# Second-half value products of a fused attention kernel in three float16 terms, with scales from a pass over v

## The chip, the cores and the metric

The kernel runs on one core of a Trainium2 chip. The metric is the device time of one execution in microseconds, lower being better; the time before is the median of three runs. The page and the trace come from one more execution, taken by the profiler. Engines are named as in the profile: PE (TensorE, matmuls), PEld (its weight loads), DVE (VectorE), ACT (ScalarE), POOL (GpSimd), SP (SyncE, which issues the transfers).

## The reference

Three stages follow each other. Causal attention over 4 batches, 8 heads, 576 positions and 64 columns per head, with a bias from a running sum; then two feed-forward layers over all 2304 tokens, with 512 columns:

```python
scores = scale * q @ k.T
cum = cumsum(maximum(s, 0))
scores = where(causal, -1e9, scores + minimum(-(cum_i - cum_j), 0))
attn = softmax(scores)                       # sum + 1e-9 below
x = attn @ v                                 # value product
h = x @ w_in                                 # 512 -> 2048
y = (s * relu(h)**2 + b) @ w_out             # 2048 -> 512
out = ((y @ w_a) * (y @ w_b)) @ w_out2       # 512 -> 1536 -> 512
```

Inputs and outputs are float32. The kernel keeps that precision by splitting operands into a high part and the rest, and by summing the products of the parts.

## The kernel before, in words

**Tiling of attention.** Heads are taken in pairs, 16 pairs for the 4 batches (`B` = 4, `NPAIR` = 4). Each pair has a first half, its first 256 query rows, which see two blocks of 128 keys (`first_half`, two pairs in each call), and a second half, its last 320 rows, which see all five blocks (`second_half`, L709). For a half, PE computes the scores, DVE takes the row maxima, ACT the exponentials, and `split_p` (L527) scales p by the reciprocal of its sum and splits it into two float16 parts. SP then issues transposes of the parts into the tile `tr`, and `value_product` (L562) multiplies.

**The value product.** v is split by `split_v` (L356) into three bfloat16 parts, p has two float16 parts. Of the six products of parts five are formed (L575), for the two heads of the pair side by side, each head in 64 of the 128 output columns. A second half has five blocks of keys with 320, 320, 320, 192 and 64 query columns, so 5 x 5 x 2 = 50 matmuls. ACT copies the sum out of PSUM, scaled back by the constant 1/32768 (L588), and DVE forms the rest (L590): the two parts of x, the input of the first feed-forward layer. The last 64 rows of each second half go to DRAM (L594) and are read back as a chunk of their own (L825).

**The first feed-forward layer.** Tokens come in nine chunks of 256: chunks 0 to 3 from the first halves, 4 to 7 from the second halves of the four batches, and chunk 8 of the short rows. Chunks 0 to 6 run as units of h (L862) and y (L882); the last two run together as `hh` (L915) and `yy` (L927). x has room for two chunks, so chunk c+2 is written where chunk c stood. The weights w1 come in 16 slices of 1 MB (L448), which ACT and DVE decode and split (L452 to L474) while the first chunks run.

**What sets the order.** All work is declared as operations with an engine, a cost and a priority (`Plan.op`, L76). `Plan.order` (L122) plays a list schedule: at each moment an engine takes the ready operation with the lowest priority number, if its buffers have room. Feed-forward matmuls have 1000 added to theirs, so attention goes first on PE and the units of h and y fill up; their element-wise work has 1000 taken off and goes first on ACT and DVE. The result is a fixed order for each engine's queue, SP's included; on the chip each queue runs in that order and waits where an input is late.

**Buffers around the change.** The tiles of the first halves (pool `att0`) are given up before those of the second halves (pool `att1`) are opened: `barrier` (L665) makes `second` (L669) follow every operation on a tile of the first pool, and the loads of the second halves (L717 to L719) come `after=opened`. In `att1` most tiles have one buffer: the raw k, q and v, the parts `vt` (L701), the transposed p (L705) and two of the three split-p tiles (L703). For each second half the parts of v are made by two ACT casts (L363) and two DVE subtractions (L365, L367).

Of the kernel before, what the change touches and what calls it, by code (L numbers as in the profile page):

```python
# [19 lines left out]
P = 128  # L20
N = 256
MASK = -1.0e30
PSC = 32768.0
G_ACT = (0, 1)
# [211 lines left out]
def fused_kernel(  # L236
# [82 lines left out]
    def make_const():  # L319
        nc.gpsimd.memset(as32(ident), 0.0)  # L320
        nc.gpsimd.affine_select(
            out=ident, in_=as32(ident), pattern=[[-1, P]], compare_op=ALU.not_equal, fill=1.0, base=0,
            channel_multiplier=1,
        )
        nc.gpsimd.memset(as32(mask1), 0.0)
        nc.gpsimd.affine_select(
            out=mask1, in_=as32(mask1), pattern=[[-1, P]], compare_op=ALU.is_ge, fill=MASK, base=0,
            channel_multiplier=1,
        )
        for i in range(0, P, SL):  # L330
            nc.gpsimd.tensor_copy(mask2[i : i + SL], as32(mask1[0:SL, 0:SL]))
# [3 lines left out]
    mask2 = atc.tile([P, SL], F32R, name="mask2")  # L335
    sb_s = const.tile([P, 1], F32, name="sb_s")
# [17 lines left out]
    t_raw = tag("att0", [P, 2, DM, 2], U32, 1, "rl")  # L354

# [134 lines left out]
    for f in range(NF1):  # L490
        if f == 1:
            sums_hl = Buf(t_w, "sums_hl")
        w1_t[f] = Buf(t_w, f"w1_{f}")
        split_w(raws[f], w1_t[f], w1[f], f % 2 == 1, W1_POS(f) - (2 * M if f >= NF1 - 3 else 0.0), W1_POS(f) - 12.0, last_rows[3:4])
        if f + 3 < NF1:
            raw_of(f + 3)
    for i in range(4, 2 * B):
        light_load(i, False)
# [62 lines left out]

    def value_product(b, half, p, vt, vap, tr, pr):  # L562
# [6 lines left out]
        xl = Buf(t_xl, f"xl{b}{p}") if half else None  # L569
        ws = [320, 320, 320, 192, 64] if half else [256, 128]  # L570

        def go():
            t = tr.t.rearrange("p (k a h q) -> p k a h q", a=2, h=2, q=nq)
            for j, w in enumerate(ws):
                for m, (vi, a) in enumerate(((0, 0), (1, 0), (2, 0), (0, 1), (1, 1))):  # L575
                    for h in range(2):
                        nc.tensor.matmul(  # L577
                            ap.t[64 * h : 64 * h + 64, :w], vap(j, h, vi), t[:, j, a, h, :w],
                            start=j == 0 and m == 0, stop=j == nkt - 1 and m == 4,
                        )  # L580

        cost = sum(5 * max(2 * w / 4.8 + 6, 58) for w in ws) / 1e3
# [4 lines left out]
        for x_, o, n in parts:  # L587
            op(ACT, ACT_PS(n), pr, lambda x_=x_, o=o: nc.scalar.activation(x_.t[:, 0], o(), AF.Copy, scale=1.0 / PSC),  # L588
               r=[ap], w=[(x_, 0)])
            op(DVE, DVE_PS(n) + 0.05, pr, lambda x_=x_, o=o: nc.vector.scalar_tensor_tensor(  # L590
                out=x_.t[:, 1], in0=o(), scalar=1.0 / PSC, in1=as32(x_.t[:, 0]), op0=ALU.mult, op1=ALU.subtract
            ), r=[ap, (x_, 0)], w=[(x_, 1)])
# [71 lines left out]

    def barrier(fn, prio):  # L665

        return op("X", 0.0, prio, fn, after=[o for o in plan.ops if any(b.tag in barrier.tags for b in o.bufs)])
# [5 lines left out]
    barrier.tags = {t_kq0, t_rv0, t_vt0, t_p0, t_tr0, t_raw, *t_hl0.values(), *t_sm0.values()}  # L673
# [27 lines left out]
    t_vt = tag("att1", [P, 5, 2, 3, D], BF16, 1, "vt")  # L701
# [7 lines left out]
    def second_half(b, p, pos):  # L709
# [27 lines left out]
        split_v((vt, lambda a: vt.t[..., a, :]), (rv, lambda: rv.t), ACT, 0.7, 0.82, pos + 0.9)  # L737
# [225 lines left out]
    def third():  # L963
# [6 lines left out]
        o for o in plan.ops if any(b.tag in att_tags or b is sets or b is masks for b in o.bufs)  # L970
# [563 lines left out]
```

## Time and profile before

| what | value |
|---|---|
| median of three runs | 1002.34 us (1001.72 to 1002.38) |
| the profiled execution | 998.96 us |
| its span in the trace | 997.2 us |
| instructions | 17243 |

The span is the time from the first to the last instruction of the profiled execution; its own time lies 1.76 us above it. In the rows below, times inside the trace count from the span's start. A group of instructions is given as line, engine, operation, output and input with their shapes, the count, then its busy time in us and the mean of one in ns, then the idle time of the engine just before and what ended it. In a chain row the first number is the start, the second the duration.

### The profile page before, as it was taken

The numbers are of one execution on the slowest core, as the hardware profiler recorded it, in microseconds if no ns is written. First come the engines' busy times: TensorE is split into PE (matmuls) and PEld (weight loads), VectorE is DVE, ScalarE is ACT, GpSimd is POOL, SyncE is SP. The second block draws the span as 40 slices with busy tenths as digits, with TensorE's granted clock in tenths as the row PEclk, the third lists the DMA queues.
The fourth block names the chain that finished last, engine by engine and source line by source line (L and its number), as shares of the span: only waits on it lengthen the run. The fifth ranks groups of instructions, "written<-read, shape, count | busy, mean of one in ns | idle before, by whom it ended". The sixth has DMA issues, their size and how long they took to land.

```text
span 997.2 us, 17243 instructions
## 1 busy us (share of the span) xinstructions
PE 968.4 (97%) x6664; PEld 871.5 (87%) x6664; DVE 707.4 (71%) x1151; ACT 548.9 (55%) x1025; POOL 108.5 (11%) x135
## 2 busy tenths in 40 slices
PE   5798999999999999999999999999999999999998
PEld 4698999999999999999988887888888888888888
DVE  6887644578888788888576627778688776878852
ACT  4788984568778777777463423344253421334431
POOL 4121000100000000000001004133143311000000
PEclk9999999999999999999999999999999999999999
DMA  9969423457776858777560103446366556977013
GB/s 240 231 164 227 163 82 79 113 128 141 168 148 157 172 128 165 159 153 146 106 226 1 63 24 125 156 147 247 137 240 228 187 185 260 377 307 253 22 65 104
DMA packets 159249, 160.12 MB, mean 161 GB/s; under 512 B 115008, under 2 KB 126016, under 8 KB 153280
## 3 DMA queue, kind: packets, MB, share of 16 engines
q1 hardware_dynamic: 159168, 159.03, 55.9%
q8 instruction: 52, 0.85, 0.4%
q14 instruction: 29, 0.24, 0.1%
HBM read 95.20 MB, written 37.52 MB: 133 GB/s over the span
## 4 chain that ended last, share of the span: by engine, by line
PE 92%; DMA 3%; DVE 2%; ACT 1%; issue 0%; POOL 0%; SPq 0%; DVEq 0%; POOLq 0%; ACTq 0%
PE b L1100 21%; PE y L882 16%; PE h L862 15%; PE pb L1324 11%; PE av L577 6%; PE hh L915 4%; PE yy L927 4%; PE bc L1100 3%; PE s L627 3%; PE s L779 3%; PE pbc L1384 2%; DMA raw<-in_w_dram 2%; DMA tr<-hl 1%; DVE x1d L1035 1%; PE s L628 0%; DMA yr<-y_dr 0%
## 5 line engine op out<-in xcount | busy, mean ns | idle before, releaser
L882 PE MATMUL y<-g,w 128*128 128x256 f32 x1344 | 183.6, 286 | 1.8 <-ACT p L643 1.8
L862 PE MATMUL h<-x_all,w 128*128 128x256 f32 x1344 | 179.0, 285 | 2.7 <-ACT x_all L588 2.1
L862 PEld LDWEIGHTS h<-x_all,w 128*128 128x128 f32 x1344 | 167.8, 192 | 4.4 <-ACT x_all L588 2.3
L882 PEld LDWEIGHTS y<-g,w 128*128 128x128 f32 x1344 | 167.9, 191 | 3.5 <-ACT p L643 2.0
L577 PE MATMUL av<-tr,vt 128*64 128x320 f16 (+4 forms) x1120 | 64.8, 273 | 9.1 <-DMA tr<-hl 9.1
L1100 PE MATMUL b<-x,wa 128*128 128x512 f32 x288 | 72.8, 390 | 0.0
L577 PEld LDWEIGHTS <-vt 128*64 128x64 bf16 x1120 | 54.3, 115 | 20.2 <-issue 6.6
L541 ACT ACTIVATE hl<-p,rc 128x256 f16<-128x256 f32 (+3 forms) x128 | 65.5, 558 | 10.7 <-DVE rc L558 6.9
L543 DVE SCALAR_TENSOR_TENSOR hl<-p,rc,hl 128x256 f16<-128x256 f32 (+3 forms) x128 | 65.5, 549 | 1.6 <-ACT hl L541 1.3
L1100 PEld LDWEIGHTS b<-x,wa 128*128 128x128 f32 x288 | 53.6, 188 | 11.3 <-ACT su L1135 0.5
L842 DVE SCALAR_TENSOR_TENSOR r<-r,sb_s 128x512 f32<-128x512 f32 x40 | 30.0, 750 | 37.8 <-ACT r L831 37.8
L1100 PE MATMUL b<-x1d,ws 128*128 128x512 f32 x216 | 54.1, 390 | 0.6 <-DVE su L1125 0.5
L1100 PE MATMUL b<-x0d,ws 128*128 128x512 f32 x216 | 53.7, 389 | 0.0
L627 PE MATMUL s<-kq 66*128 66x256 f32 (+1 forms) x128 | 42.4, 458 | 10.2 <-DMA kq<-sums 7.8
L1324 PE MATMUL pb<-g,wo 128*128 128x512 f32 x216 | 50.7, 390 | 0.0
L1100 PEld LDWEIGHTS b<-x1d,ws 128*128 128x128 f32 x216 | 40.4, 188 | 9.7 <-DVE su L1125 1.4
L1324 PEld LDWEIGHTS pb<-g,wo 128*128 128x128 f32 x216 | 40.4, 188 | 8.7 <-DVE g L1272 0.4
L1100 PEld LDWEIGHTS b<-x0d,ws 128*128 128x128 f32 x216 | 40.4, 188 | 8.3
L463 DVE SCALAR_TENSOR_TENSOR raw<-raw 128x1024 uint32<-128x1024 uint32 x28 | 34.9, 1245 | 17.1 <-ACT raw L457 14.2
L831 ACT ACTIVATE r<-h 128x512 f32<-128x512 f32 x56 | 33.5, 598 | 24.1 <-PE h L862 22.1
L1125 DVE TENSOR_TENSOR su<-b,su 128x512 f32<-128x512 f32 x48 | 33.0, 688 | 17.9 <-PE b L1100 17.7
L915 PE MATMUL hh<-x_all,w 128*128 128x512 f32 x192 | 45.7, 389 | 0.0
(380 smaller groups left out, 1881.3 us busy)
## 6 DMA issues: line engine op xcount, KB each, us to landing
raw<-in_w_dram SPq DMA_DIRECT2D x16, 1024.0 KB
raw<-in_w2ab_dram SPq DMA_DIRECT2D x12, 1024.0 KB
ab_dr<-at_all SPq DMA_DIRECT2D x24, 512.0 KB
R<-ab_dr SPq DMA_DIRECT2D x24, 512.0 KB
wo<-wo_dr SPq DMA_DIRECT2D x12, 1024.0 KB
rk<-in_k_dram SPq DMA_DIRECT2D x16, 576.0 KB
raw_o<-in_w2o_dram SPq DMA_DIRECT2D x6, 1024.0 KB
wo_dr<-wao SPq DMA_DIRECT2D x24, 256.0 KB
```

The source lines that it names most:

```text
L463: op(DVE, 1.15, pr, lambda: nc.vector.scalar_tensor_tensor(out=hi(), in0=hi(), scalar=3, in1=lo(), op0=ALU.logical_shift_left, op1=ALU.bit ...
L541: nc.scalar.activation(o, i_, AF.Copy, scale=r_)
L543: nc.vector.scalar_tensor_tensor(out=o, in0=i_, scalar=r_, in1=place()[:, k0:k1, 0, :cols], op0=ALU.mult, op1=ALU.subtract)
L577: nc.tensor.matmul(ap.t[64 * h : 64 * h + 64, :w], vap(j, h, vi), t[:, j, a, h, :w], start=j == 0 and m == 0, stop=j == nkt - 1 and m == 4,)
L627: nc.tensor.matmul(o, qt[:66, x, h, ti * P : (ti + 1) * P], kt[:66, x, h, :w], start=True, stop=False)
L831: op(ACT, 0.49, e, lambda: nc.scalar.activation(r.t.rearrange("p a n -> p (a n)"), hp.t, AF.Relu), r=[hp], w=[r], late=0.1)
L862: nc.tensor.matmul(o, w[:, wi, c, :], x_t[ck, c].t[:, xi], start=m == 0, stop=m == 3 * KC - 1)
L882: nc.tensor.matmul(o, w1_t[2 * fp + j].t[:, 1, wi, e * P : (e + 1) * P], g.t[:, gi, j], start=fp == 0 and e % 2 == 0 and j == wi == gi == ...
L915: nc.tensor.matmul(hp.t, w[:, wi, c, :], x_all[:, :, c, xi, :], start=m == 0, stop=m == 3 * KC - 1)
L927: nc.tensor.matmul(y_ps[e].t, w1_t[f].t[:, 1, wi, e * P : (e + 1) * P], g.t[:, gi].rearrange("p a n -> p (a n)"), start=f == m == 0, stop= ...
L1100: nc.tensor.matmul(o, wt.t[:, q, wi, kt * P : (kt + 1) * P], hl_of(kt, xi), start=first and n == 0, stop=last and n == 5, skip_group_check ...
L1324: nc.tensor.matmul(banks[bi][dp].t, wv(i2, wi, dp), hl.t[:, i2, xi, :], start=n_ in fresh and ip == i2 == m == 0, stop=ip == NIP - 1 and i ...
```

## The change

The second halves' v is split into two float16 parts instead of three bfloat16 parts. Their value product takes three products of parts instead of five. For float16's range v is scaled first, by one factor for batches 0 and 1 and one for batches 2 and 3: the largest absolute value over all v of these batches, made into a factor by a matmul with a constant matrix `total`, which adds up the 128 partitions. The factor and its inverse (with the old constant in it) lie in `vsc`, a column per use, and take the place of constants in ACT's and DVE's operations. The maxima come from a pass over v: 16 loads of 320 KB into a tile `vm` with one buffer, each followed by a maximum on DVE. The loads may be issued once the sixth load from the end of w1 has been (`behind=w1_last`); their priorities, 110 to 170, come after those of the first halves. The first halves keep their five terms. The tile `vm` belongs to the first pool, and so to the operations that the opening of the second pool follows.

```diff
+VSC = 32768.0
...
     def make_const():
+        nc.gpsimd.memset(total, 1.0 / VSC)
...
+    vmax = atc.tile([P, B * NPAIR + 2], F32, name="vmax")
+    vsc = atc.tile([P, 2, 2], F32, name="vsc")
...
+    t_vm = tag("att0", [P, 5, 2, D], F32, 1, "vm")
...
+    w1_last = [o for o in plan.ops if o.eng == SP][-6:][:1]
...
     def value_product(b, half, p, vt, vap, tr, pr):
+        terms = ((0, 0), (1, 0), (0, 1)) if half else ((0, 0), (1, 0), (2, 0), (0, 1), (1, 1))
+        back = vsc[:, b // 2, 1:2] if half else 1.0 / PSC
...
-                for m, (vi, a) in enumerate(((0, 0), (1, 0), (2, 0), (0, 1), (1, 1))):
+                for m, (vi, a) in enumerate(terms):
...
-            op(ACT, ACT_PS(n), pr, lambda x_=x_, o=o: nc.scalar.activation(x_.t[:, 0], o(), AF.Copy, scale=1.0 / PSC),
-               r=[ap], w=[(x_, 0)])
+            op(ACT, ACT_PS(n), pr, lambda x_=x_, o=o: nc.scalar.activation(x_.t[:, 0], o(), AF.Copy, scale=back),
+               r=[ap, *([(vsc_b, b // 2)] if half else [])], w=[(x_, 0)])
...
+    def v_max(i, pr):
+        vm = Buf(t_vm, f"vm{i}")
+        op(SP, 0.4, pr, lambda: nc.sync.dma_start(vm.t, v[i // NPAIR, i % NPAIR]), w=[vm], dma=327680, behind=w1_last)
+        op(DVE, 0.8, pr, lambda: nc.vector.tensor_reduce(
+            out=vmax[:, i : i + 1], in_=vm.t.rearrange("p c h d -> p (c h d)"), axis=AX.X, op=ALU.max, apply_absolute_value=True
+        ), r=[vm], w=[(vmax_b, i)], late=0.1)
+    def v_scale(z, pr):
+        n = B * NPAIR // 2
+        i, sc = 2 * n + z, vsc[:, z]
+        op(DVE, 0.2, pr, lambda: nc.vector.tensor_reduce(
+            out=vmax[:, i : i + 1], in_=vmax[:, z * n : (z + 1) * n], axis=AX.X, op=ALU.max
+        ), r=[(vmax_b, z * n + j) for j in range(n)], w=[(vmax_b, i)])
+        bank = Buf(t_s, f"vbank{z}")
+        op(PE, 0.1, pr, lambda: nc.tensor.matmul(bank.t[:, :1], total, vmax[:, i : i + 1], start=True, stop=True),
+           r=[(vmax_b, i), masks], w=[bank], late=0.1, slack=True)
+        def go():
+            nc.vector.tensor_scalar_max(sc[:, 0:1], bank.t[:, :1], 1e-30)
+            nc.vector.tensor_scalar_mul(sc[:, 1:2], sc[:, 0:1], 1.0 / PSC)
+            nc.vector.reciprocal(sc[:, 0:1], sc[:, 0:1])
+        op(DVE, 0.5, pr, go, r=[bank], w=[(vsc_b, z)])
+    for z in range(2):
+        for i in range(z * B * NPAIR // 2, (z + 1) * B * NPAIR // 2):
+            v_max(i, 110.0 + 4.0 * i)
+        v_scale(z, 110.0 + 32.0 * (z + 1))
...
-    barrier.tags = {t_kq0, t_rv0, t_vt0, t_p0, t_tr0, t_raw, *t_hl0.values(), *t_sm0.values()}
+    barrier.tags = {t_vm, t_kq0, t_rv0, t_vt0, t_p0, t_tr0, t_raw, *t_hl0.values(), *t_sm0.values()}
...
-    t_vt = tag("att1", [P, 5, 2, 3, D], BF16, 1, "vt")
+    t_vt = tag("att1", [P, 5, 2, 2, D], F16, 1, "vt")
...
-        split_v((vt, lambda a: vt.t[..., a, :]), (rv, lambda: rv.t), ACT, 0.7, 0.82, pos + 0.9)
+        op(ACT, 0.7, pos + 0.9, lambda: nc.scalar.activation(vt.t[..., 0, :], rv.t, AF.Copy, scale=vsc[:, b // 2, 0:1]),
+           r=[rv, (vsc_b, b // 2)], w=[(vt, 0)])
+        op(DVE, 0.82, pos + 0.9, lambda: nc.vector.scalar_tensor_tensor(
+            out=vt.t[..., 1, :], in0=rv.t, scalar=vsc[:, b // 2, 0:1], in1=vt.t[..., 0, :], op0=ALU.mult, op1=ALU.subtract
+        ), r=[rv, (vsc_b, b // 2), (vt, 0)], w=[(vt, 1)])
```

The DVE operation of the copy out of PSUM (L590) takes `back` in the same way.

## Rows read from the trace of the kernel before

**Rows 1.** The page's part 1: busy us, share of the span, instructions.

```profile
PE 968.4 (97%) x6664; PEld 871.5 (87%) x6664; DVE 707.4 (71%) x1151; ACT 548.9 (55%) x1025; POOL 108.5 (11%) x135
```

**Rows 2.** The page's part 4: the chain that ended last, by engine and by line.

```profile
PE 92%; DMA 3%; DVE 2%; ACT 1%; issue 0%; POOL 0%; SPq 0%; DVEq 0%; POOLq 0%; ACTq 0%
PE b L1100 21%; PE y L882 16%; PE h L862 15%; PE pb L1324 11%; PE av L577 6%; PE hh L915 4%; PE yy L927 4%; PE bc L1100 3%; PE s L627 3%; PE s L779 3%; PE pbc L1384 2%; DMA raw<-in_w_dram 2%; DMA tr<-hl 1%; DVE x1d L1035 1%; PE s L628 0%; DMA yr<-y_dr 0%
```

**Rows 3.** Busy time by stretch: PE, PEld, DVE, ACT, POOL, clock, DMA share, GB/s.

```profile
229.00:299.50 70.50, 70.50 (x671) 67.76 (x672) 58.44 (x122) 54.75 (x118) 0.82 (x4) 1.00 0.75 157
```

**Rows 4.** The chain in order of time: start us, us, what.

```profile
229.03 2.73 PE av L577 x50
...
299.53 2.73 PE av L577 x50
...
491.64 2.73 PE av L577 x50
```

**Rows 5.** Busy time of line L577 alone, second halves: PE, PEld, clock, DMA share, GB/s.

```profile
229.00:494.40 265.40, 44.71 (x800) 37.52 (x800) 1.00 0.71 152
```

**Rows 6.** Groups by form, 229 to 299.5 us; the last row 95 to 193 us.

```profile
L363 ACT CAST vt<-rv 128x640 bf16<-128x640 f32 x8 | 5.8, 725 | 3.0 <-PE av L577 3.0
...
L365 DVE TENSOR_TENSOR rv<-rv,vt 128x640 f32<-128x640 f32 x4 | 3.3, 826 | 1.8 <-ACT vt L363 1.8
...
L541 ACT ACTIVATE hl<-p,rc 128x512 f16<-128x512 f32 x8 | 5.7, 719 | 0.0
...
L543 DVE SCALAR_TENSOR_TENSOR hl<-p,rc,hl 128x512 f16<-128x512 f32 x8 | 5.9, 747 | 0.0
...
L588 ACT ACTIVATE x_all<-av 128x256 fp32r<-128x256 f32 x4 | 1.5, 374 | 0.0
...
L541 ACT ACTIVATE hl<-p,rc 128x256 f16<-128x256 f32 x11 | 5.2, 509 | 0.5 <-ACT p L643 0.5
```

**Rows 7.** SP's issues in order of time: start us, us, line, what.

```profile
94.68 40.96 SPq L448 DMA_DIRECT2D raw<-in_w_dram  x6
```

**Rows 8.** The chain again: waits for loads of 256 KB.

```profile
612.46 3.97 DMA yr<-y_dr
...
623.08 2.62 DMA yrc<-y_dr
```

**Rows 9.** Groups by form, 229 to 299.5 us: maxima and mask products.

```profile
L784 DVE TENSOR_REDUCE nm<-s 128x1 f32<-128x512 f32 x8 | 5.2, 687 | 0.5
...
L780 PE MATMUL s<-mask,ident 128*128 128x128 f32 x16 | 3.6, 223 | 0.0
```

**Rows 10.** Busy time by stretch while the first chunks run.

```profile
100.00:125.00 25.00, 23.21 (x193) 23.21 (x194) 15.66 (x24) 25.00 (x49) 0.00 (x0) 1.00 0.43 161
...
125.00:150.00 25.00, 25.00 (x210) 25.00 (x210) 11.94 (x16) 20.88 (x29) 0.00 (x0) 1.00 0.22 80
...
150.00:175.00 25.00, 25.00 (x261) 23.87 (x260) 11.28 (x25) 12.42 (x35) 2.47 (x4) 1.00 0.40 82
```

**Rows 11.** DVE and PE in order of time: w1's last slice.

```profile
145.17 1.23 DVE L472 TENSOR_TENSOR w<-raw,w 128x1024 fp32r<-128x1024 f32 x1
...
147.97 1.60 PE L862 MATMUL h<-x_all,w 128*128 128x256 f32 x12
```

**Rows 12.** PE in order of time: its first matmul.

```profile
7.79 1.19 PE L627 MATMUL s<-kq 66*128 66x256 f32 x2 [7.79 <-DMA kq<-sums]
```

**Rows 13.** POOL in order of time: first use of the second pool.

```profile
193.70 0.74 POOL L689 MEMSET Q<- 64x768 f32 x1 [31.19 <-PE av L577]
```

**Rows 14.** ACT and PE in order of time: chunk 4's last input, its first h.

```profile
285.30 0.38 ACT L588 ACTIVATE x_all<-av 128x256 fp32r<-128x256 f32 x1
...
297.93 1.60 PE L862 MATMUL h<-x_all,w 128*128 128x256 f32 x12
```

**Rows 15.** SP and PE in order of time: short rows read back, the last chunks.

```profile
499.26 3.19 SPq L825 DMA_DIRECT2D x_all<-xl_dr  x4
...
508.79 3.59 PE L915 MATMUL hh<-x_all,w 128*128 128x512 f32 x15
```

More of the change, by code (lines that the diff above doesn't have):

```diff
@@ L335, in fused_kernel @@
     mask2 = atc.tile([P, SL], F32R, name="mask2")
+    total = atc.tile([P, P], F32, name="total")
+    vmax = atc.tile([P, B * NPAIR + 2], F32, name="vmax")
+    vsc = atc.tile([P, 2, 2], F32, name="vsc")
     sb_s = const.tile([P, 1], F32, name="sb_s")
@@ L560, in recip @@
         op(DVE, (3 if add_first else 2) * 0.17, pr, lambda: go(rc.t[:, 0:1] if add_first else rc.t), r=[sm], w=[rc])
+    vmax_b, vsc_b = Buf(None, "vmax", 1), Buf(None, "vsc", 1)
     def value_product(b, half, p, vt, vap, tr, pr):
@@ L578, in go @@
                             ap.t[64 * h : 64 * h + 64, :w], vap(j, h, vi), t[:, j, a, h, :w],
-                            start=j == 0 and m == 0, stop=j == nkt - 1 and m == 4,
+                            start=j == 0 and m == 0, stop=j == nkt - 1 and m == len(terms) - 1,
                         )
-        cost = sum(5 * max(2 * w / 4.8 + 6, 58) for w in ws) / 1e3
+        cost = sum(len(terms) * max(2 * w / 4.8 + 6, 58) for w in ws) / 1e3
         op(PE, cost, pr, go, r=[vt, tr], w=[ap], late=0.15, mode=1, room=[xt])
@@ L587, in value_product @@
         for x_, o, n in parts:
-            op(ACT, ACT_PS(n), pr, lambda x_=x_, o=o: nc.scalar.activation(x_.t[:, 0], o(), AF.Copy, scale=1.0 / PSC),
-               r=[ap], w=[(x_, 0)])
+            op(ACT, ACT_PS(n), pr, lambda x_=x_, o=o: nc.scalar.activation(x_.t[:, 0], o(), AF.Copy, scale=back),
+               r=[ap, *([(vsc_b, b // 2)] if half else [])], w=[(x_, 0)])
             op(DVE, DVE_PS(n) + 0.05, pr, lambda x_=x_, o=o: nc.vector.scalar_tensor_tensor(
-                out=x_.t[:, 1], in0=o(), scalar=1.0 / PSC, in1=as32(x_.t[:, 0]), op0=ALU.mult, op1=ALU.subtract
-            ), r=[ap, (x_, 0)], w=[(x_, 1)])
+                out=x_.t[:, 1], in0=o(), scalar=back, in1=as32(x_.t[:, 0]), op0=ALU.mult, op1=ALU.subtract
+            ), r=[ap, (x_, 0), *([(vsc_b, b // 2)] if half else [])], w=[(x_, 1)])
         if half:
@@ L969, in fused_kernel @@
     ready2 = [op("X", 0.0, 0.0, third, after=[
-        o for o in plan.ops if any(b.tag in att_tags or b is sets or b is masks for b in o.bufs)
+        o for o in plan.ops if any(b.tag in att_tags or b in (sets, masks, vsc_b, vmax_b) for b in o.bufs)
     ])]
```

## The prediction, made before the result

> **What bounds the kernel now.** I read the busy times first: TensorE (PE) is busy for 968.4 of a span of 997.2 us [rows 1]. The chain that ended last says the same, PE holds 92% of it, and the value product (`av`, L577) alone is 6% [rows 2]. So work taken off PE shortens the kernel wherever PE has no gap, and the question is whether it has none where the second halves run. The table by stage answers that. From 229.0 to 299.5 us PE is busy for the whole 70.50 us, with VectorE (DVE) at 58.44, ScalarE (ACT) at 54.75 and a granted clock of 1.00, the 2.4 GHz level [rows 3]; the next two stretches of 70.5 us repeat that row. The stretch is one batch of second halves: its first value product starts at 229.03, that of the next batch at 299.53, and the sixteenth and last at 491.64 [rows 4]. That is 17.6 us for each second half, of which 2.73 us are its value product and the rest its scores and the two feed-forward units (h and y) that the list schedule puts between. PE is never idle there, so whatever a second half needs less of it comes off the end, provided that the feed-forward work always finds its inputs.
>
> The Trainium skill ("Perfetto Trace Analysis", Identifying the Most-Contended Engine) says that matmul busy time is not a good measure for TensorE, because its matmuls are pipelined, and tells the reader to look at the weight loads. By that rule the stage could have another limit than PE, which is rival B below; here weight loads are busy for 67.76 of 70.50 us [rows 3], so on this count the trace sides with PE.
>
> **The value product, second halves.** Five terms become three, so 50 matmuls become 30 in each of 16 halves. All 800 of them were recorded [rows 5], all in this stage, and the chain shows 2.73 us for each 50 [rows 4]. Every k-tile loses the same two of five, whatever its width, so I scale: 2.73 x 2/5 = 1.09 us, times 16 = **17.5 us less PE time**. A float16 stationary operand has no row: v was bfloat16 here, and only the moving operand was float16. If such a load were no faster or slower the sum stands; rival E prices the other case. Below, the saving could be the busy time alone, 44.71 us x 2/5 = 17.9 [rows 5].
>
> **Splitting v.** Now: two ACT casts of 725 ns and two DVE subtractions of some 826 ns a half [rows 6]. After: one ACT operation with a scale read per partition, and one three-operand DVE operation. The nearest rows do just this to p: 719 ns on ACT and 747 on DVE for 512 columns [rows 6]; for 640 columns that is at most 5/4 of it, 0.90 and 0.93 us, and not under the 0.72 and 0.82 of the present ones. So a half saves 0.55 to 0.73 us of ACT and 0.71 to 0.83 of DVE. Neither is the bound, so I count 0; but both lie on the loop of a second half (the cast waits until the last value product has let go of v's parts, and the splitting of p is queued behind it on ACT), so the loop gets shorter, not longer.
>
> **Scaling back.** The copies out of PSUM (L588, L590) now take their scale from a [128,1] operand. An ACT operation on 256 columns with such a scale took 509 ns, the copy with a constant 374 [rows 6]; between 0 and 0.14 us each, four ACT and DVE operations a half, and nothing in PE's way: 0. ScalarE's own saving shrinks by it to some 0.3 us a half. The Trainium skill ("ScalarE: Activation LUTs", What ACT_TABLE_LOAD costs) gives 93 ns for each such operand, a rule against this change. By its figure the price is an estimated 0.09 us a copy instead of my bound of 0.14, and a little less shortening of the loop in rival B; no row has the two forms side by side.
>
> **The pass over v.** It adds 16 loads of 320 KB on SP's queue, 16 DVE maxima of 640 columns, and two scale steps, each one DVE maximum, one PE matmul of one column and three short DVE operations. It may start when the load of w1's slice 10 is issued, the first of the last six, whose issues run from 94.68 to 135.64 us [rows 7]. With one buffer the pass is a chain: load, maximum, next load. The nearest loads, of 256 KB, landed in 2.62 and 3.97 us [rows 8]; for 320 KB at most 5/4: 2.6 to 5.0. A maximum is 0.69 us at 512 columns [rows 9], so 0.86 at most; with 0.5 for issue and hand-over a link takes 4.0 to 6.4 us, and 16 of them 64 to 102 us. The pass ends between 159 and 197 us; I take 180. What hides it: from 100 to 175 us DMA is busy for 22 to 43%, and DVE for 15.66, 11.94 and 11.28 of each 25 us [rows 10], so 5.2 MB and 14 us of maxima find room. What is queued behind: on SP, a load that waits for the one buffer holds up the w1 loads and the transposes of the first halves; on DVE, a maximum that waits for its load holds up the decoding of w1 (L463, L472), for which ACT, full at 25.00 of 25, is the clock until 125 us. The last w1 slice is written from 145.17 to 146.40 and PE takes up h at 147.97 [rows 11]: 1.6 us of slack, the thinnest cover here. A hold-up of one maximum behind one load, 0 to 3 us, thus costs PE 0 to 1.4; I take 0.7, the middle.
>
> The two matmuls: a 128-column mask product took 223 ns [rows 9]; one column of plain float32 has no row, so I put it between half and four times that, 0.1 to 0.9 us, and PE, in order, waits there for the maximum before it: 0 to 2 us each. I take 0.2 each, 0.4 together, since each is scheduled well after its last maximum at low priority. The memset of `total` delays POOL at the start, where the mask has time: PE's first matmul starts at 7.79 us, after a load [rows 12]. I count 0.
>
> **Opening the second halves' buffers.** They now also wait for the pass. They open at 193.70, after the last value product of the first halves [rows 13]. A pass that ends by then costs nothing; ending at 197 delays them by 3 us. What is late next: chunk 4 of the feed-forward, whose first h starts at 297.93, while its last input is written from 285.30 on [rows 14]: 11.6 us of lead (after some 1 us of the DVE's part), 0 on the end.
>
> **Sum.** The profiled execution took 998.96 us (span 997.2): 998.96 - 17.5 + 0.7 + 0.4 = 982.6. The median of the runs shown, 1002.34, is 3.4 above it; I expect the same of the new kernel, and forecast **986.0 us**, 1.6% faster. A measurement of this kernel tells some 0.2% (2 us) from no change.
>
> **Rivals.**
> **B, the loop of a second half sets the pace.** One buffer each for v's parts, the transposed p and two of the split-p tiles ties a value product to the next through ACT, DVE and the transposes. If it stays at 17.6 us while PE needs 16.5, the feed-forward work catches up and PE starves before the end. Then the last value product still ends near 493.3 us; two copies (about 1 us), the store of the short rows (2.62), four loads (3.19 to issue, 2.62 to land) put the last pair of chunks at 502.7 instead of 508.79 [rows 4, 8, 15]: 6 us gained, 997 us. For it: ACT's cast waits for `av` for 3.0 us a batch [rows 6]. Against it: that very wait ends with `av`, now 1.09 us earlier.
> **C, slower: the opening waits for the pass.** If a link takes 8.2 us (each load behind a 1 MB w1 load or a transpose), the pass ends at 94.7 + 131 = 226 us, 32 us after today's opening. Of these the lead of chunk 4 covers 11.6; the other 20.4 on PE outweigh the 16.4 gained: **1006 us**. The point from which it decides is 28 us of delay (11.6 + 16.4); below, it only eats the gain. Against it: 5.0 us is the longest I can make of a load, 6.4 of a link.
> **D, the pass disturbs w1.** Several of the last five w1 loads or decodings fall behind a load of v, 2.6 to 5.0 us each, against 1.6 us of slack: 3 to 10 us given back, some 991 us.
> **E, the terms do not get cheaper.** If a pair of matmuls with float16 v took 182 instead of 2.73 / 25 = 109 ns, three terms would cost what five do: 1003.4 us, no change. Nothing in the trace speaks for it but the missing row.
>
> **How the numbers follow.** Forecast (all of the gain but 0 to 3 us) 0.75; B 0.09; D 0.09; E 0.03; C 0.04. Faster by over 0.2% is the forecast, B and D: 0.93; within 0.2% E: 0.03; slower C: 0.04. The low end is the sum with no price for the pass and 17.9 for the terms: 984.4, less 1 for a list order that falls out otherwise downstream: 983.4. The high end takes in most of D: 994. B, E and C are left out, 0.16.
>
> **What would show it.** Right: `av` x30 at 1.64 us on the chain, batches 66 us apart with PE still full, 480 second-half records, and the end of the chunk stage (508.79) some 16 us earlier, with everything after it shifted by as much. The pass ends before 194 us and no PE wait names its buffer or `vmax`. Wrong: PE gaps ahead of h in the second-half stage or before the last two chunks (B, C), PE or DVE waits for w1 or v's loads between 95 and 195 us (D), `av` x30 near 2.7 us (E).

## The result, and the profile after

The changed kernel took **988.1 us**, the median of four runs (987.19 to 988.42), where the kernel before took 1002.36 beside it: a ratio of **0.9857 [0.984, 0.9875]**, 14.3 us less. The profiled execution took 988.12 us with a span of 986.3. The forecast of 986.0 lies 2.1 us below, and the range of 983.4 to 994 holds it. In a later batch the same two kernels stood at 989.72 and 1000.71, a ratio of 0.9894 [0.9876, 0.9912]: there only 11.0 us less. The two intervals do not overlap, so a difference of 0.4% between batches proves nothing by itself. I take the gain as 11 to 14 us, against the 16.4 that I forecast.

The page's parts 1 and 4 of the changed kernel (busy us, share, instructions; the chain by engine):

```profile
PE 953.8 (97%) x6348; PEld 859.2 (87%) x6348; DVE 712.3 (72%) x1159; ACT 544.6 (55%) x1009; POOL 108.6 (11%) x136
...
PE 86%; DMA 6%; DVE 3%; ACT 2%; issue 1%; SPq 0%; POOL 0%; DVEq 0%; ACTq 0%; POOLq 0%
```

Against [rows 1, 2]: PE is busy for 14.6 us less, the span is only 10.9 shorter. The difference, 3.7 us, is PE's idle time: 997.2 - 968.4 = 28.8 us before, 986.3 - 953.8 = 32.5 now. PE's share of the chain fell from 92 to 86%, and other engines and DMA took it. Where PE was freed and where it stands idle is the reading below.

The second halves' value products alone (line L588, once L577), from the first to the last: PE, PEld, clock, DMA share, GB/s. It answers to [rows 5].

```profile
232.20:481.70 249.50, 28.06 (x480) 23.77 (x480) 1.00 0.76 157
```

The chain in order of time, which answers to [rows 4] (start us, us, what; the start of an `av` is that of its first recorded matmul):

```profile
232.32 1.68 PE av L588 x30
...
299.62 1.68 PE av L588 x30
...
366.89 1.68 PE av L588 x30
...
479.92 1.68 PE av L588 x30
...
487.38 9.83 DMA x_all<-xl_dr
```

A value product takes 1.68 us in place of 2.73, and all 16 together 28.06 in place of 44.71: **16.65 us less**. A batch takes 67.30 us (299.62 - 232.32), and the next 67.27, in place of 70.50. But the first value product starts 3.3 us later than before (229.03), and at the end a transfer stands on the chain, which [rows 2] don't have among their larger entries: the reading back of the short rows. PE's own waits from 90 to 500 us say the same (what it waited for, us, times, longest):

```profile
PE hh L960 <- DMA x_all<-xl_dr: 1.2, 1, 1.2
PE av L588 <- DMA tr<-hl: 1.1, 1, 1.1
PE av L588 <- ACT Q L769: 0.8, 1, 0.8
PE av L588 <- issue: 0.6, 1, 0.6
```

Before, none of these four was there. The second lies at 166 us in the first halves; the third and fourth lie in the second-half stage, where PE had no gap at all [rows 3]. They add up to 3.7 us, as much as PE's idle time grew by. Not all of it comes from the pass: a kernel without it (below) has gaps in the stage and at hh too. The table by stage shows the first and third batch of second halves (busy PE, PEld, DVE, ACT, POOL, clock, DMA share, GB/s):

```profile
232.30:299.60 67.30, 66.56 (x591) 64.68 (x592) 56.37 (x118) 53.60 (x114) 0.82 (x4) 1.00 0.77 164
...
366.90:433.30 66.40, 66.40 (x590) 64.23 (x592) 56.29 (x118) 53.72 (x114) 0.85 (x4) 1.00 0.82 166
```

PE is full in the third and 0.74 us short of it in the first. Last, the new forms, 229 to 295 us (line, engine, operation, shapes, count, busy us, mean ns, idle before), which answer to [rows 6]:

```profile
L778 ACT ACTIVATE vt<-rv,vsc 128x640 f16<-128x640 f32 x4 | 3.3, 824 | 0.0
...
L599 ACT ACTIVATE x_all<-av,vsc 128x256 fp32r<-128x256 f32 x4 | 1.9, 476 | 1.2 <-PE av L588 1.1
...
L780 DVE SCALAR_TENSOR_TENSOR vt<-rv,vsc,vt 128x640 f16<-128x640 f32 x4 | 3.5, 879 | 0.0
```

The split takes 0.82 us of ACT and 0.88 of DVE a half, in place of 2 x 0.725 and some 2 x 0.826.

**The pass.** Its loads are issued from 94.7 to 174.0 us, a link of 5.3 us, and its last maximum ends at 179.44. Work beside it moved. Shown are the last slice of w1 and the last maximum on DVE, the opening on POOL, and on SP the transposes and the first load of a second half (start us, us, line; one fence for each engine):

```profile
149.93 1.23 DVE L478 TENSOR_TENSOR w<-raw,w 128x1024 fp32r<-128x1024 f32 x1 [1.79 <-ACT w L477]
...
178.63 0.81 DVE L680 TENSOR_REDUCE vmax<-vm 128x1 f32<-128x640 f32 x1
```

```profile
198.84 0.74 POOL L730 MEMSET Q<- 64x768 f32 x1 [32.03 <-DMA rq<-in_q_dram]
```

```profile
184.76 9.17 SPq L664 DMA_TRANSPOSE tr<-hl  x3
193.99 0.57 SPq L758 DMA_DIRECT2D rk<-in_k_dram  x1
```

w1's last slice is written by 151.16 instead of 146.40 [rows 11], 4.8 us later, and the opening comes at 198.84 instead of 193.70 [rows 13], 5.1 later, though the pass was over 19 us before it. SP's two largest waits from 90 to 190 us:

```profile
SPq L679 <- DMA vm<-in_v_dram: 31.8, 10, 7.4
SPq L679 <- DVE vmax L680: 14.7, 13, 3.4
```

For 46.5 of some 80 us SP stood at a load of v, waiting for the one buffer, and all that it had to issue behind it, w1's loads and the transposes of the first halves, waited with it. That this made the two shifts is argued, not shown: all of SP's waits in this stretch add up to 69.5 us here and to 74.2 before, of which 37.4 were for w1's buffers. SP did not wait longer than before; it waited for something else.

### The profile page after: what moved, and what is told of

Read it like the earlier page. It is cut to its first block, busy times and chain, and to the rows that moved or that the text cites. A ratio compares the mean times of both kernels' runs of the same rounds, so it can differ in the third digit from the quotient of the medians.

```text
span 986.3 us, 16627 instructions
## 1 busy us (share of the span) xinstructions
PE 953.8 (97%) x6348; PEld 859.2 (87%) x6348; DVE 712.3 (72%) x1159; ACT 544.6 (55%) x1009; POOL 108.6 (11%) x136
## 4 chain that ended last, share of the span: by engine, by line
PE 86%; DMA 6%; DVE 3%; ACT 2%; issue 1%; SPq 0%; POOL 0%; DVEq 0%; ACTq 0%; POOLq 0%
PE b L1145 20%; PE y L927 15%; PE h L907 15%; PE pb L1369 11%; PE av L588 5%; PE hh L960 4%; PE yy L972 4%; PE bc L1145 3%; PE s L638 3%; PE s L824 3%; PE pbc L1429 2%; DMA raw<-in_w_dram 2%; DMA x_all<-xl_dr 1%; DMA tr<-hl 1%; DMA R<-ab_dr 1%
## 5 line engine op out<-in xcount | busy, mean ns | idle before, releaser
L927 PE MATMUL y<-g,w 128*128 128x256 f32 x1344 | 181.5, 286 | 1.8 <-ACT p L654 1.7
L907 PE MATMUL h<-x_all,w 128*128 128x256 f32 x1344 | 178.1, 286 | 0.9 <-DVE x_all L601 0.3
L588 PE MATMUL av<-tr,vt 128*64 128x320 f16 (+4 forms) x800 | 48.1, 275 | 13.0 <-ACT hl L548 6.1
L588 PEld LDWEIGHTS <-vt 128*64 128x64 f16 (+1 forms) x800 | 40.5, 117 | 21.4 <-issue 9.2
L972 PE MATMUL yy<-gg,w 128*128 128x512 f32 x192 | 45.6, 389 | 0.0
```

What stands on the lines that cost most here:

```text
L588: nc.tensor.matmul(ap.t[64 * h : 64 * h + 64, :w], vap(j, h, vi), t[:, j, a, h, :w], start=j == 0 and m == 0, stop=j == nkt - 1 and m == l ...
L907: nc.tensor.matmul(o, w[:, wi, c, :], x_t[ck, c].t[:, xi], start=m == 0, stop=m == 3 * KC - 1)
L927: nc.tensor.matmul(o, w1_t[2 * fp + j].t[:, 1, wi, e * P : (e + 1) * P], g.t[:, gi, j], start=fp == 0 and e % 2 == 0 and j == wi == gi == ...
L972: nc.tensor.matmul(y_ps[e].t, w1_t[f].t[:, 1, wi, e * P : (e + 1) * P], g.t[:, gi].rearrange("p a n -> p (a n)"), start=f == m == 0, stop= ...
```

## The experiments

The theory that I set out with: PE's freed time is the gain, the pass takes back a little. The rivals: the loop of a second half sets the pace (B), the pass is what decides (C, D). All times in one place; before is the kernel before, run on the same chip beside them; rows with the same time in that column ran on one chip.

| kernel | us (runs) | before | ratio [95%] |
|---|---|---|---|
| three terms alone | 994.98 (6) | 999.75 | 0.9951 [0.9934, 0.9968] |
| lighter split alone, five terms | 999.87 (12) | 1000.35 | 0.9998 [0.9988, 1.0009] |
| both, without the pass | 985.01 (5) | 999.75 | 0.9838 [0.9821, 0.9854] |
| pass alone | 1001.95 (12) | 999.75 | 1.0026 [1.0015, 1.0038] |
| change, pass behind all of w1 | 1015.1 (4) | 1000.35 | 1.0145 [1.0128, 1.0162] |
| change, short rows read back first | 987.04 (4) | 1000.35 | 0.9862 [0.9844, 0.988] |
| change, finer pass and short rows first | 985.0 (5) | 1000.35 | 0.9838 [0.9817, 0.9859] |
| the change again | 989.72 (5) | 1000.71 | 0.9894 [0.9876, 0.9912] |
| change, finer pass | 986.23 (5) | 1000.71 | 0.9864 [0.9843, 0.9884] |
| change, finer pass and short rows first, again | 985.35 (4) | 1000.71 | 0.9849 [0.9832, 0.9865] |
| both, no pass, constant scales | 982.83 (5) | 1000.71 | 0.9842 [0.9817, 0.9866] |

### Three terms alone

The kernel before with three of the five products; the other two are left out, and the three bfloat16 parts of v are still made.

```diff
+        terms = ((0, 0), (1, 0), (0, 1)) if half else ((0, 0), (1, 0), (2, 0), (0, 1), (1, 1))
...
-                for m, (vi, a) in enumerate(((0, 0), (1, 0), (2, 0), (0, 1), (1, 1))):
+                for m, (vi, a) in enumerate(terms):
```

> The kernel before with only three of the five terms in the second halves' value products; v keeps its three bfloat16 parts, two casts and two subtractions, and there is no pass. It leaves two products out of the sum. Theory 1 (PE is the bound and 16.7 us of its time went): 985 to 987 us, value products of 30 matmuls at 1.68 us. Theory 3 (the loop of a second half sets the pace and got shorter mostly through the lighter split): over 990 us, with PE gaps of several us ahead of value products or h.

Only 4.8 us came of it, though PE's time for these products fell as in the change (each is 1.68 us here too). The value products start 17.34 us apart on average ((487.02 - 226.87) / 15), nearly the 17.5 of before, so the feed-forward work caught up with them. The first and the last of them:

```profile
226.87 1.75 PE L578 MATMUL av<-tr,vt 128*64 128x320 f16 x30
...
487.02 1.75 PE L578 MATMUL av<-tr,vt 128*64 128x320 f16 x30
```

PE's largest waits from 220 to 510 us:

```profile
PE hh L916 <- DMA x_all<-xl_dr: 8.9, 1, 8.9
PE av L578 <- DMA tr<-hl: 1.7, 1, 1.7
```

PE waits at only two of the sixteen value products (1.7 us here, 0.5 for ACT's p at another). What fills the 17.34 us is h and y work that the fixed order puts between, so the pace is that of the list schedule, which plays the loop with its own costs. Whether the chip could run this loop faster in another order was not tried.

At the end PE has no h or y left and waits for the last short rows; then it also runs at a lower clock, and its first 12 hh matmuls take 4.69 us, where the change's take 2.98. The stretch by the table (busy PE, PEld, DVE, ACT, POOL, clock, DMA share, GB/s):

```profile
495.00:505.00 10.00, 3.50 (x8) 2.84 (x9) 6.91 (x9) 6.34 (x6) 0.00 (x0) 0.50 0.80 286
```

That is rival B as I had drawn it, for this half of the change: hh starts at 501.50 (I had worked out 502.7) and the kernel gains 4.8 us (I had 6).

### The lighter split alone, and both without the pass

Both have the float16 split, with the scales as columns that POOL sets to constants at the start, and no pass. The first forms five products, two of them twice; the second is the change in all else.

```diff
+        nc.gpsimd.memset(vsc[:, :, 0:1], VS)
+        nc.gpsimd.memset(vsc[:, :, 1:2], 1.0 / (VS * PSC))
...
-    for z in range(2):
...
+        terms = ((0, 0), (1, 0), (0, 1), (0, 0), (1, 0)) if half else ((0, 0), (1, 0), (2, 0), (0, 1), (1, 1))
```

The last line is in the first of the two alone.

> The lighter split alone: v in two scaled float16 parts with constant scales and no pass, but five terms again in the second halves (two of the three are formed twice, so the sum is off). One cast and one DVE operation a half less than before, PE as before. Theory 1 (PE is the bound, the lighter split only keeps a second half's loop short enough): no change against before, within 0.2%, batches of 70.5 us, PE full. Theory 3 (the split is a gain by itself): 3 us or more faster than before.

> The changed kernel without the pass: the scale columns are set once by POOL to a constant (1024 and its inverse), all else as changed, the scales still read per partition. Theory 1: 2 to 5 us faster than the changed kernel, 983 to 986 us, first value product of the second halves near 229 us again. Theory 2: 987 to 989 us, since the lead that the pass uses up is not needed.

The lighter split alone changes nothing that can be measured (0.9998). Its value products come closer together all the same, 16.90 us apart ((483.82 - 230.26) / 15) with all five terms: the split sets their pace, and PE, still full, sets the end. On top of the three terms it is worth 994.98 - 985.01 = **10.0 us**, on one chip. The groups by form of the kernel with three terms and the old split, 229 to 295 us, show what it replaces:

```profile
L363 ACT CAST vt<-rv 128x640 bf16<-128x640 f32 x8 | 5.8, 724 | 2.0 <-DVE rv L365 1.3 <-PE av L578 0.7
...
L365 DVE TENSOR_TENSOR rv<-rv,vt 128x640 f32<-128x640 f32 x4 | 3.3, 820 | 0.0
...
L367 DVE TENSOR_TENSOR vt<-rv,vt 128x640 bf16<-128x640 f32 x4 | 3.3, 816 | 0.0
```

A half's cast, subtraction, cast, subtraction follow each other, 3.1 us in all; in the change cast and remainder take 0.82 + 0.88 = 1.7. So the two parts of the change are worth -0.5 (on another chip) and -4.8 us alone and -14.7 together.

Without the pass the first value product starts at 229.31, and they come 16.56 us apart. PE's waits from 200 to 510 us in this kernel:

```profile
PE av L585 <- DMA tr<-hl: 1.9, 2, 1.6
PE hh L927 <- DMA x_all<-xl_dr: 1.3, 1, 1.3
```

So gaps in the second-half stage and a wait at hh, as the change has them, come without the pass too.

### The pass alone

The kernel before with the pass added, its scales not used: old split, five terms, constant scaling.

```diff
+    t_vm = tag("att0", [P, 5, 2, D], F32, 1, "vm")
...
+    for z in range(2):
+        for i in range(z * B * NPAIR // 2, (z + 1) * B * NPAIR // 2):
+            v_max(i, 110.0 + 4.0 * i)
+        v_scale(z, 110.0 + 32.0 * (z + 1))
```

> The kernel before plus the whole pass over v (loads, maxima, scale steps, the opening that waits for it), with the old three bfloat16 parts, five terms and constant scale. Theory 1 (the pass is most of what was given back: in the changed kernel w1's last slice was ready 4.8 us and the second pool 5.1 us later): 1 to 5 us slower than before, 1003.5 to 1007. Theory 2 (the pass hides, and the shortfall lies in the second halves' own loop and in the end of the chunk stage): within 1 us of before, 1001.5 to 1003.3, with w1 late by the same 4 to 5 us but PE without a gap between 125 and 200 us.

The pass costs 0.26% here, 2.6 us, as theory 1 said. PE's only wait from 90 to 515 us is 1.1 us for a transpose of the first halves, the same as in the change at 166 us; where the rest of the 2.6 sits, no wait shows. Its trace has the same two shifts as the changed kernel's, on DVE and on POOL:

```profile
151.46 1.23 DVE L478 TENSOR_TENSOR w<-raw,w 128x1024 fp32r<-128x1024 f32 x1 [1.82 <-ACT w L477]
```

```profile
201.13 0.74 POOL L730 MEMSET Q<- 64x768 f32 x1 [31.92 <-DMA rq<-in_q_dram]
```

In the changed kernel the price is the difference to the kernels without it. By the ratios of two batches it is 0.9857 - 0.9838, 1.9 us, with intervals that overlap; on one chip, beside the version with constant scales below, it is 989.72 - 982.83 = 6.9 us, with intervals that don't. I take 2 to 7.

### The pass behind all of w1

```diff
-    w1_last = [o for o in plan.ops if o.eng == SP][-6:][:1]
+    w1_last = [o for o in plan.ops if o.eng == SP][-1:]
```

> The changed kernel with the pass over v held back until w1's last slice is being loaded (behind the last load instead of the sixth from the end). w1 should be ready as early as before, but the pass then ends near 205 to 220 us, and the second pool opens 10 to 26 us later than before. Theory C (the opening of the second pool has 11.6 us of lead and then costs PE one for one): 988 to 1000 us, PE gaps ahead of h of chunk 4 or of value products, more the later it opens. Rival (the lead is larger, since the second halves catch up): 985 to 988, no such gap.

14.7 us slower than before, by the ratios 25 to 29 us above the change, and outside what either theory gave: the end that rival C had, by another way. w1 is undisturbed (its last slice written by 146.69), but on SP the second halves' loads now stand behind six loads of v:

```profile
189.40 21.63 SPq L679 DMA_DIRECT2D vm<-in_v_dram  x6
211.08 0.42 SPq L758 DMA_DIRECT2D rk<-in_k_dram  x1
```

The opening itself is not late, POOL clears the first Q at 193.83. The first value product starts at 251.95, and the last at 503.79: the loop doesn't run faster for being late (16.79 us apart). PE's longest wait from 200 to 530 us, and the stretch after it:

```profile
PE hh L960 <- DMA x_all<-xl_dr: 15.1, 1, 15.1
```

```profile
510.00:525.00 15.00, 3.48 (x8) 2.81 (x9) 6.22 (x9) 6.13 (x6) 0.00 (x0) 0.50 0.76 277
```

The first load of a second half is issued at 189.69 in the kernel before, at 193.99 in the change, at 211.08 here. The last step of 17.1 us cost 25.7 us of span (1012.0 - 986.3), some of it at the lower clock. So 21.4 us of delay have used up more than the whole gain, where I had worked out 28. Where between the gain would end can't be read off a line through these traces: the finer pass below issues that load at 196.33, later than the change, and is faster.

### The short rows read back first

The last chunk's rows are read back ahead of the next stage's weights and rows on SP.

```diff
+        xlast = op(SP, 0.4, 431.0, lambda p=p: nc.sync.dma_start(as32(x_t[NCK - 1, p].t), as32(xl_dr.t[p])),
...
+        words = decode(raw, src, n % 2 == 1, pos, pos, [xlast])
...
+                       r=y_rows(2 * j + T, 2 * kh + kt), w=[(t, T)], dma=262144, behind=[xlast])
```

> The changed kernel with the reading back of the last chunk's rows issued ahead of the loads of the next stage's weights and rows. Theory 1 (the 1.2 us wait of the last two chunks for x_all is transfers queued ahead of it): that wait is gone and the end of the chunk stage 1 to 1.5 us earlier. Rival (the second halves come too late): the wait stays at 1 us or more.

SP's queue in the changed kernel, where the read-back comes after four row loads and two weight loads of 1 MB:

```profile
483.74 0.52 SPq L605 DMA_DIRECT2D xl_dr<-xl  x1
484.31 2.02 SPq L1099 DMA_DIRECT2D yr<-y_dr  x4
486.37 0.90 SPq L454 DMA_DIRECT2D raw<-in_w2ab_dram  x2
487.38 2.24 SPq L870 DMA_DIRECT2D x_all<-xl_dr  x4
```

With it first, PE's wait ahead of hh is gone, hh starts at 492.72, but 24 y matmuls that stood ahead of it now follow, and the second-half stage has gaps of up to 1.15 us (at 313.2; in the change up to 0.8). Alone it is worth nothing that the intervals show (0.9862 and 0.9857, from two batches).

### What reading the scale costs

The kernel without the pass, its scale columns replaced by constants in the operations.

```diff
-        back = vsc[:, b // 2, 1:2] if half else 1.0 / PSC
+        back = 1.0 / (VS * PSC) if half else 1.0 / PSC
```

> The changed kernel without the pass, and with constant scales in the operations of ACT and DVE themselves instead of scales read per partition from a column. Beside the kernel without the pass but with the columns (985.01 us, ratio 0.9838 to before) this tells what reading the scale costs. My step counted it at 0 for the end: within 1 us of that ratio, and the copy out of PSUM on ACT shorter by 0 to 0.14 us in the groups. A rival: the loop of a second half is shorter by the price of four such reads, 0.4 us a half, and the time falls by up to 2 us.

Groups by form, 229 to 295 us, with the constants:

```profile
L741 ACT ACTIVATE vt<-rv 128x640 f16<-128x640 f32 x4 | 3.0, 738 | 1.3 <-PE av L581 1.3
...
L592 ACT ACTIVATE x_all<-av 128x256 fp32r<-128x256 f32 x4 | 1.5, 374 | 0.1
```

and with the columns (no pass either):

```profile
L745 ACT ACTIVATE vt<-rv,vsc 128x640 f16<-128x640 f32 x4 | 3.3, 826 | 2.2 <-PE av L585 2.2
...
L596 ACT ACTIVATE x_all<-av,vsc 128x256 fp32r<-128x256 f32 x4 | 1.8, 460 | 0.1
```

86 and 88 ns more for each ACT operation, inside my bounds of 0 to 0.14 us; on DVE 820 became 881 and 422 became 481. The Trainium skill ("ScalarE: Activation LUTs", What ACT_TABLE_LOAD costs) gives some 93 ns for such an operand: the runs agree, with 86 and 88. On the end no difference shows: 0.9842 and 0.9838, on two chips.

### A finer pass, and the version that beats both

The pass in 32 loads of three and two blocks with two buffers, behind the last but one load of w1; once alone, and twice with the short rows read back first, the first time on another chip. The unaltered change ran beside the other two.

```diff
-    t_vm = tag("att0", [P, 5, 2, D], F32, 1, "vm")
+    t_vm = tag("att0", [P, 3, 2, D], F32, 2, "vm")
...
-    w1_last = [o for o in plan.ops if o.eng == SP][-6:][:1]
+    w1_last = [o for o in plan.ops if o.eng == SP][-2:][:1]
...
+        for c, n in ((0, 3), (1, 2)):
```

> The end of the chunk stage as in the tail kernel, and the pass in 32 loads of three or two blocks with two buffers, behind the last but one load of w1, so that a load runs while DVE takes the maximum before it. Theory 1 (the pass costs some 2 us by delaying w1 and the opening, the end 1.2): the pass ends before 190 us, w1's last slice within 2 us of before, and the kernel takes 2 to 3 us less than the changed one. Rival (what was given back lies in the list order): no more than 1 us less.

> The changed kernel once more, unaltered, beside the next three on one chip. Its ratio to the kernel before has been 0.9857 [0.984, 0.9875]; I expect 0.984 to 0.987 again, thus 987 to 989 us where the kernel before takes 1002.4. If the 3.4 us between the profiled execution of before and the median of its runs come from the dip of the granted clock after the gap at 84 to 86 us, this kernel's profiled execution should lie within 1 us of its own median, as in its first run (988.12 beside 988.1).

> The changed kernel with the pass over v alone altered: 32 loads of three or two blocks with two buffers, behind the last but one load of w1 instead of the sixth from the end; the read-back at the tail as in the change. The pass costs the change 2 to 2.6 us by its two measurements. If that cost is the hold-up of w1's last slices and of the opening (4.8 and 5.1 us later), this form gives 1.5 to 2.5 us back: ratio to the changed kernel 0.9975 to 0.9985, w1's last slice written by 150.5 us and the opening by 194.5. If it is the work of the pass itself (maxima on DVE, traffic), wherever it stands, the time stays within 0.7 us of the changed kernel.

> As the run before, with the short rows read back ahead of the next stage's loads too (the kernel that took 985.0 us on another chip), here beside the changed kernel itself. If the read-back is worth its 1.2 us of waiting at the last pair of chunks, this is 1 to 1.5 us under the run before; if the feed-forward work just fills the same time elsewhere (as with the read-back alone: 987.04 against 988.1), under 0.7 us.

The finer pass took 986.23 us beside 989.72, a little more than the 1.5 to 2.5 us expected, though the two intervals touch (0.9843 to 0.9884, and 0.9876 to 0.9912). Its w1 is written by 149.98 and the opening comes at 193.79, within what the hold-up theory said; on SP the wait for v's loads to land fell from 28.9 us (the change, in the same batch) to this, from 90 to 200 us:

```profile
SPq L680 <- DVE vmax L682: 15.6, 16, 3.7
SPq L680 <- DMA vm<-in_v_dram: 9.7, 8, 2.9
```

and PE has only three waits left between 90 and 530 us, none in the second-half stage:

```profile
PE y L930 <- ACT p L654: 1.8, 1, 1.8
PE hh L963 <- DMA x_all<-xl_dr: 0.3, 1, 0.3
PE av L588 <- DMA tr<-hl: 0.2, 1, 0.2
```

That does not make the hold-up the cause. In the same batch the change wrote w1's last slice by 148.91, 1.1 us sooner than the finer pass, and its first load of a second half is issued sooner too (the finer pass, then the change):

```profile
196.33 0.42 SPq L761 DMA_DIRECT2D rk<-in_k_dram  x1
```

```profile
192.40 0.57 SPq L758 DMA_DIRECT2D rk<-in_k_dram  x1
```

Only the opening is earlier than the change's (197.26 there), and the first value product starts at 233.53, for 230.67 in the change. What went away are gaps of PE: its waits from 90 to 530 us add up to 2.3 us, in the change to 5.1, and in the two kernels without any pass to 5.4 (scale columns) and 1.9 (constants), so the gaps come and go without a pass too. The order of the list changed with the pass, the value products come 16.34 us apart ((478.58 - 233.53) / 15), and three things were altered at once: the size of the loads, the buffers and the start. Which of them gave the 3.5 us back, and how much of it lies in the list order, as the rival had it, stays open.

That the pass ends late is no harm as such: its last maximum starts at 198.9. My expectation of an end before 190 us in the first of these runs was wrong: there the last one started at 198.6, and w1's last slice came 4.0 us later than in the kernel before, not within 2. With the short rows first as well it took 985.35 us, all four runs (983.91 to 986.08) under all five of the change (987.15 to 991.18), and its interval, 0.9832 to 0.9865, lies clear of the change's on that chip, 0.9876 to 0.9912. **This is the fastest version that keeps the pass**: 0.4% below the change. The read-back's own share of it, 0.9 us, is not told from nothing. The unaltered change's profiled execution lay 2.6 us under its own median, not within the 1 us that I expected.

### The kernel before once more

> The kernel before, unchanged, for a second trace: the first one belongs to an execution 3.4 us shorter than the median. Theory 1: the 3.4 us sit in one place that the changed kernel also has or has not, most likely a wait for transfers around 600 to 630 or 840 to 860 us. Rival: they are spread over the whole span by a shift of all engines.

One run, 1001.35 us. The first traced execution of this kernel (998.96) had a granted clock of 1.00 all through; here, after PE had stood idle for 2.11 us, the clock falls (PE in order of time; then the table by stretch):

```profile
86.52 0.39 PE L862 MATMUL h<-x_all,w 128*128 128x256 f32 x1 [2.11 <-ACT x_all L588]
```

```profile
85.00:90.00 5.00, 3.25 (x11) 2.69 (x12) 4.76 (x12) 4.53 (x11) 1.01 (x1) 0.73 1.16 206
90.00:95.00 5.00, 5.00 (x28) 5.00 (x28) 3.33 (x7) 3.74 (x10) 1.84 (x2) 0.59 1.05 138
```

hh starts at 511.13 instead of 508.79, 2.3 us later, and the execution is 2.4 us longer. The dip need not be all of it: the value product before the gap starts at 82.12 here and at 80.23 there, so this execution was 1.9 us late already. In the changed kernel's first trace the two gaps there are 0.30 and 0.33 us, and the clock stays at 1.00. That is a pattern. The four traces of kernels with five terms wait 1.7 to 2.4 us at that place, and the clock falls in three of them; the ten with three terms wait 0.7 us or less, and it stays at 1.00 from 80 to 95 us. Nothing that the change adds runs there, and why the wait differs is open; a part of the gain by medians may come from it. But over the 43 runs of before on these three chips, those whose mean clock was 0.997 or less (30 of them) averaged 1000.5 us and the others 999.8. The dip is at most a part of the 3.4 us that lay between the first profiled execution and the median.

## Why the prediction was right, and where it was not

**Right: the value product and its place.** 2.73 x 3/5 was taken as 1.64 us, and 1.68 came: 1.05 us less for each in place of 1.09, 16.65 in place of 17.5 in all. The float16 operand that had no row (rival E) costs nothing that shows: 1.68 us with either form of v. The last value product starts at 479.92 in place of 491.64, so 11.7 of the 16.7 us had come off by then. Of the signs that I had named, the batches came 67.3, 67.3 and 66.4 us apart in place of 66, and two signs of being wrong came, both small: the gap of 1.2 us before the last two chunks, and DVE's waits for v's loads (up to 2.98 us, at 155.46).

**Wrong, and the step that matters: "Splitting v ... I count 0".** I counted the split at nothing because neither ACT nor DVE was the bound, and put the loop of a second half down as a rival with 0.09. The runs show that the loop, as the list schedule plays it, is a bound of its own, close behind PE: with three terms and the old split it takes 17.34 us a half where PE needs about 16.5, the value products keep the old pace, and 10 us of the gain stay out. The lighter split costs or saves nothing while five terms keep PE busy (0.9998) and is a condition of the gain once they don't. The sentence that the loop "gets shorter, not longer" was right, and was the reason why rival B did not come about; but the term belonged into the sum as what lets the 17.5 through, not as 0. In the changed kernel the value products come 16.5 us apart, about what PE needs, with three gaps in the stage (1.5 us) that the version with the finer pass, at 16.34, has not.

**Mis-sized: the pass.** I had 0.7 + 0.4 us; it costs 2.6 on its own (1.0026) and 2 to 7 in the change. Its length was right (180 taken, 179.44 measured; a link of 5.3 between 4.0 and 6.4). The two matmuls took 0.28 us each, with no wait ahead of them. What I mispriced is the queue: "a hold-up of one maximum behind one load, 0 to 3 us" was one hold-up, where SP stood at v's loads for 46.5 us in all. w1's last slice came 4.8 us later (slack 1.6), but PE did not lose it there; it lost 1.15 us at 166 us, waiting for a transpose of the first halves. That is all of the price that a wait of PE shows for sure, since gaps in the stage and at hh came without the pass too. The second halves' first load went out 4.3 us later, but the finer pass, with 6.6, is faster. Where the rest of the price sits stays open. Rival D, with 3 to 10 us given back, was near in size, but not by w1: PE waited 0.3 us for it, and 0.4 before.

**Wrong: "Opening ... 0 on the end", and rival C's point of decision.** I let the lead of chunk 4 (11.6 us) stand for slack. The late pass shows where it ends: 21.4 us of delay of the second halves' first load went through the loop, which did not catch up, to the last value product and the reading back of the short rows, and there PE had run out of h and y. The finer pass shows that 6.6 us need not cost more than the change's 4.3. Between the two nothing was measured. The lead of one chunk's input is not the slack of the stage when the stock of other work is finite and the loop runs at its own pace.

**Not foreseen: the tail.** I said the end of the chunk stage would come some 16 us earlier; it came 11.45 earlier (497.34 for 508.79, [rows 15]). The read-back of the short rows, off the chain before, takes 9.83 us on it now, and hh waits 1.2. One kernel without the pass has that wait too (1.3 us), the one with constant scales has none. I had that path in rival B's working and not in the forecast's.

**The offset.** I carried over the 3.4 us between the profiled execution and the median; the change showed 0.0 in its first batch and 2.6 in its second. By traces alone the change is worth 10.9 us of span, by medians 14.3 and 11.0. My 986.0 came near because a sum that was 5.5 us too good (16.4 less the 10.9) met an offset that was 3.4 too high: two errors that partly cancelled. In the span's 10.9, 16.7 of the value products stand against 3.7 of new idle time and some 2 us by which PE's busy time fell less than theirs did (14.6 for 16.7). The two new matmuls are 0.6 of these 2; the rest I can't place, since by the pages h (179.0, now 178.1) and y (183.6, now 181.5) did not grow.

## What to carry to other kernels

When work is taken off the engine that is full, work out how long the dependent loop beside it takes without that engine, and put the slower of the two into the sum: a saving on an engine that is "not the bound" can be the condition under which the main saving counts. If the order is fixed beforehand, that pace is the one that the schedule plays, so look for it there too. A pass that hides in every engine's free time can still cost: price what queues behind its waits, and try it in smaller transfers with a second buffer and another start, as those together paid here. A chunk's lead is slack only as long as there is other work to fill it with to the very end.

## What the runs showed of the hardware

PE's clock fell to its lower level (1.2 of 2.4 GHz, a granted 0.50 over whole stretches) after waits of 9 and 15 us at hh. After one of 2.11 us at 84 us it was 0.73 and 0.59 over two stretches of 5 us; a gap of 2.05 us at the same place in the other trace of the same kernel left it at 1.00 (ahead of the h at 84.57). So nearly the same gap was followed by a dip in one execution and not in the other. The prices that had no row before: a one-column float32 matmul took 0.28 us for a pair of records (two bounds were 0.1 and 0.9), a maximum over 640 columns 0.82, and an operand read per partition 86 to 88 ns on ACT and some 60 on DVE.
